# Top-k attention and a low-rank mixer on one core: VectorE and GpSimd put in program order, and some VectorE work moved to GpSimd and ScalarE

## The chip, the cores and the metric

The kernel runs on one core of a Trainium2 chip. A core has TensorE (PE: matmuls, results into PSUM), VectorE (DVE), ScalarE (ACT) and GpSimd (POOL), each with its own instruction queue that is worked off in order, SyncE (SP) which issues most of the DMAs, and SBUF as working memory. Engines wait for one another only through semaphores. The metric is device microseconds of one execution.

## The reference

Eight batches, eight heads, a sequence of 576, a head dimension of 64, all in float32:

```
scores = scale * q @ k^T                       # 576 x 576 per head
kth    = the 32nd largest score of each row
attn   = softmax over the scores >= kth, 0 elsewhere
x      = attn @ v, heads side by side          # (8, 576, 512)
h      = x^T @ U @ V                           # mixes along the sequence, rank 32
u      = x + h^T
out    = u + relu(u @ w_ch1) @ w_ch2           # 512 -> 2048 -> 512
```

U, V, w_ch1 and w_ch2 arrive as float64 and are rounded to float32 in the kernel, by integer operations on their two words.

## The kernel before

The work goes by *pairs* of heads (32 of them, four to a batch) and by *steps*: a pair has five steps, four with 128 rows of queries of both heads (two chunks of 128 x 576 scores) and a fifth with the last 64 rows of both (one chunk). Step n is `divmod(n, 5)`; there are 160.

A step passes these functions. `scores` (from L261 on) computes the scores into PSUM, and ACT copies them to SBUF as `Ssb`. `front` (from L297 on) finds the 32nd largest on VectorE in four rounds: a MAX8 gives the next eight maxima, a MATCH_REPLACE8 strikes them out (L315, L327, L331). The softmax mask of the first chunk is VectorE's (L335), that of the second POOL's (L333, L334), each beside an exponential on ACT (L295; for the second chunk after its mask). `turns` transposes the weights on TensorE (L363, L368), ACT copies them out of PSUM as `PT`. `values` multiplies with v (L383 to L396). When a pair is done, `mixed` transposes its result, scales it by 1/sum into `x` (VectorE, L419, straight out of PSUM), and computes u (pT, Tb, up). When a batch's four pairs are done, `mlp` is appended to the `fillers`: 256 accumulating matmuls, two instructions each in the trace (L467, L486), relu on ACT, and for each of eight tiles the sum `oT` (VectorE, L499, out of PSUM) that `turned_back` transposes, copies to `ob` and stores.

One PSUM pool of two buffers (`ps_t`, tag `tp`) serves all transposes, `O`, `pT` and `up`; another of two serves the MLP.

The order of the work: the main loop runs over the steps and calls these generators in turn. `fill` does a share of MLP matmuls between the pieces of a step, eight times a step; a step of one chunk counts 0.65. The MLP of a batch thus runs beside the attention of the next batch; in the first 21 steps (`n <= ALONE`) there is none to do, and behind the last attention step one batch's MLP is left. `next_params(1)` moves the rounding of weights on by a slab of 128 x 512: it joins the slab before (L160 and L168 on VectorE, L172 on POOL), prepares the one that has arrived (L152, L154 on ACT, L153 on POOL) and loads the next into one of three `raw` buffers. It is called once a step up to step 20 and twice a step after that; there are 36 slabs.

TensorE's and ACT's queues are in the order in which the program calls them:

```python
    ctx.enter_context(tc.manual_schedule(engines={PE, ACT}))
```

The order on VectorE and POOL is that of a scheduler, which takes operations when it thinks them ready, the ones under `high_priority` first; `last_mask` pins a slab's join behind a step's L335 and the next step's first maximum behind the join's first operation.

## Time and profile before

| | |
|---|---|
| runs | 1918.98 us median of 3 (1918.07 to 1920.71) |
| the profiled execution | 1917.73 us, of which the span from first to last instruction is 1915.9 |
| busy of the span | TensorE 1772.1 us, VectorE 1654.0, ACT 953.4, POOL 571.8 |
| granted TensorE clock | 0.958 of full speed, mean |
| the chain that ended last | TensorE 63%, VectorE 26%, ACT 4%, POOL 3% |

The profile is of one execution. "Busy" is time in which an engine had an instruction; the granted clock is that of TensorE, as a share of 2.4 GHz (0.5 is the lower level, 1.2 GHz). A wait is put down to the instruction that ended it. The chain follows the work back from the last instruction, at each point to what released it or to the instruction before it on its engine. Busy shares over the whole span mix stretches with different limits, so the rows further down go by stretch. Line numbers are those of the kernel before.

### The profile page before, as it was taken

The page shows a single profiled execution, that of the slowest core. Times are in us where ns is not written, and L with a number is a line of the kernel's source. Part 1 is how long each engine was busy: PE and PEld are TensorE (multiplying, and loading weights), DVE is VectorE, ACT ScalarE, POOL GpSimd, SP SyncE. Part 2 cuts the span into 40 slices and gives each one's busy share as a digit, 9 for nine tenths or more (in the row PEclk, how much of TensorE's full clock was granted, in tenths as well). Part 3 has the DMA queues.
Part 4 walks back from the last instruction along what each step waited for, and adds up shares of the span by engine and source line. Part 5 has one row for each costly group of instructions (what it writes and reads, how often), then busy time and mean ns, then how long its engine had stood idle before and what let it go on. Part 6 is the DMA issues. An engine that isn't in the chain of part 4 may idle for free.

```text
span 1915.9 us, 29112 instructions
## 1 busy us (share of the span) xinstructions
PE 1772.1 (92%) x10528; PEld 1335.0 (70%) x10528; DVE 1654.0 (86%) x3433; ACT 953.4 (50%) x2345; POOL 571.8 (30%) x346
## 2 busy tenths in 40 slices
PE   5666688999899999999999999999999999999999
PEld 3444465687667877778677877778677877778777
DVE  7999998999999989999899999999899998997000
ACT  4555555554554545555555546555555545554111
POOL 3545556422332222222232222222232222232000
PEclk7767698999999999999999999999999999999999
DMA  2222222201001010100001010101001010000000
GB/s 72 72 60 59 68 74 79 58 17 28 23 20 30 24 30 15 27 18 23 25 20 30 23 31 15 27 15 26 25 20 31 22 31 15 15 8 7 6 14 11
DMA packets 127296, 58.21 MB, mean 30 GB/s; under 512 B 89905, under 2 KB 124977, under 8 KB 127153
## 3 DMA queue, kind: packets, MB, share of 16 engines
q1 hardware_dynamic: 125952, 56.06, 11.0%
q8 instruction: 83, 1.36, 0.3%
q14 instruction: 61, 0.49, 0.1%
q10 hardware_dynamic: 1200, 0.30, 0.1%
HBM read 46.89 MB, written 9.44 MB: 29 GB/s over the span
## 4 chain that ended last, share of the span: by engine, by line
PE 63%; DVE 26%; ACT 4%; issue 3%; POOL 3%; DMA 1%; DVEq 0%; SPq 0%; POOLq 0%; ACTq 0%
PE mm L467 21%; PE mm L486 18%; DVE rr L327 11%; DVE m L331 10%; PE sc L270 6%; PE O L396 5%; PE tp L363 4%; DVE first L315 2%; DVE E L335 2%; PE O L383 1%; PE up L442 1%; ACT E L295 1%; POOL E L333 1%; PE O L393 1%; PE tp L251 1%
## 5 line engine op out<-in xcount | busy, mean ns | idle before, releaser
L331 DVE MAX8 m<-rr 128x8 f32<-128x576 f32 x864 | 614.9, 747 | 4.0
L333 POOL TENSOR_SCALAR E<-Ssb,m 128x576 f32<-128x576 f32 x128 | 285.6, 2231 | 1089.2 <-DVE m L331 546.3
L467 PE MATMUL mm<-uT,w 128*128 128x256 f32 (+1 forms) x2048 | 559.7, 411 | 2.7 <-ACT hT L479 2.7
L486 PE MATMUL mm<-hT,w 128*128 128x256 f32 (+1 forms) x2048 | 560.4, 411 | 0.0
L467 PEld LDWEIGHTS mm<-uT,w 128*128 128x128 f32 x2048 | 364.0, 191 | 110.2 <-issue 30.5
L486 PEld LDWEIGHTS mm<-hT,w 128*128 128x128 f32 x2048 | 364.2, 191 | 100.2 <-issue 22.9
L327 DVE MATCH_REPLACE8 rr<-m,rr 128x576 f32<-128x576 f32 x576 | 427.8, 743 | 0.0
L315 DVE MAX8 first<-Ssb 128x8 f32<-128x576 f32 x288 | 215.6, 752 | 58.6 <-ACT Ssb L290 58.5
L364 ACT COPY PT<-tp 128x512 f32<-128x512 f32 x288 | 168.5, 585 | 187.1 <-PE tp L363 185.2
L363 PE MATMUL tp<-ident,E 128*128 128x128 f32 x1152 | 185.4, 286 | 81.3 <-ACT E L295 54.3
L363 PEld LDWEIGHTS tp<-ident,E 128*128 128x128 f32 x1152 | 144.7, 146 | 145.5 <-ACT E L295 69.1
L295 ACT ACTIVATE E<-Ssb,nmax 128x576 f32<-128x576 f32 x288 | 223.3, 776 | 11.2 <-POOL Ssb L334 5.9
L270 PE MATMUL sc<-qkT 64*128 64x288 f32 (+1 forms) x1280 | 213.9, 457 | 0.4 <-ACT qkT L252 0.4
L327 DVE MATCH_REPLACE8 rr<-first,Ssb 128x576 f32<-128x576 f32 x288 | 212.3, 742 | 0.0
L334 POOL TENSOR_TENSOR Ssb<-Ssb,E 128x576 f32<-128x576 f32 x128 | 188.0, 1469 | 10.6
L405 ACT COPY XT<-O 128x128 f32<-128x128 f32 x128 | 34.2, 267 | 248.9 <-PE O L396 248.9
L479 ACT ACTIVATE hT<-mm 128x320 f32<-128x320 f32 (+1 forms) x256 | 104.3, 408 | 106.7 <-PE mm L467 105.2
L499 DVE TENSOR_TENSOR oT<-uT,mm 128x320 f32<-128x320 f32 (+1 forms) x64 | 28.4, 444 | 146.4 <-PE mm L486 146.4
L396 PE MATMUL O<-PT,va 128*64 128x128 f32 x2048 | 154.2, 298 | 0.0
L270 PEld LDWEIGHTS sc<-qkT 64*128 64x128 f32 (+1 forms) x1280 | 111.2, 189 | 53.9 <-issue 27.3
L335 DVE SCALAR_TENSOR_TENSOR E<-Ssb,m,E 128x576 f32<-128x576 f32 x160 | 130.5, 815 | 18.5 <-ACT E L295 9.9
L396 PEld LDWEIGHTS O<-PT,va 128*64 128x64 f32 x2048 | 120.7, 147 | 17.1 <-issue 3.6
(68 smaller groups left out, 1378.1 us busy)
## 6 DMA issues: line engine op xcount, KB each, us to landing
raw<-in_moe_w_ch_dram SPq DMA_DIRECT2D x32, 512.0 KB, 3.8
ld_q<-in_q_dram SPq DMA_DIRECT2D x64, 128.0 KB, 2.8
va<-in_v_dram SPq DMA_DIRECT2D x64, 128.0 KB, 2.4
out_dram<-ob SPq DMA_DIRECT2D x64, 128.0 KB, 1.9
ld_k<-in_k_dram SPq DMA_DIRECT2D x62, 128.0 KB, 2.8
ld_ends<-in_q_dram SPq DMA_DIRECT2D x32, 32.0 KB, 2.2
vd<-in_v_dram SPq DMA_DIRECT2D x64, 16.0 KB, 2.0
vt<-in_v_dram SPq DMA_DIRECT2D x32, 32.0 KB, 2.3
```

Source lines behind the costliest of these rows:

```text
L270: nc.tensor.matmul(sc[slice(0, n) if t < NT else half(h), h, 0:HALF], lhsT=qkT[half(h), 0, cols(t)], rhs=qkT[half(h), 1, i * HALF : (i + 1 ...
L295: nc.scalar.activation(E, chunk, AF.Exp, bias=nmax, scale=SCALE, accum_out=total)
L315: ins = nc.vector.max(ms[c], curs[c])
L327: nc.vector.match_replace(nxt, ms[c], curs[c], NEG)
L331: nc.vector.max(ms[c], curs[c])
L333: nc.gpsimd.tensor_scalar(Es[1], chunks[1], ms[1][:, 7:8], NEG, ALU.is_lt, ALU.mult)
L334: nc.gpsimd.tensor_tensor(chunks[1], chunks[1], Es[1], ALU.add)
L335: ins = nc.vector.scalar_tensor_tensor(out=Es[0], in0=chunks[0], scalar=ms[0][:, 7:8], in1=Es[0], op0=ALU.is_ge, op1=ALU.mult, accum_out=s ...
L363: nc.tensor.transpose(tp[:, j, :], E2[:, a : a + P], ident)
L396: nc.tensor.matmul(O[half(h)], lhsT=va[:, h, j, :], rhs=PT[:, NT * h + j], start=False, stop=(j == NT - 1),)
L467: nc.tensor.matmul(ph[:, 0:w], lhsT=w1[:, cc, f * P : (f + 1) * P], rhs=uT[:, cc, lo:hi], start=(cc == 0), stop=(cc == NC - 1),)
L486: nc.tensor.matmul(po[:, 0:w], lhsT=w2[:, f, c * P : (c + 1) * P], rhs=hTs[f][:, 0:w], start=(f == 0), stop=(f == NF - 1),)
```

## The change

VectorE and POOL are now also in program order; the scheduler places nothing. A step's rounds are given out in pieces: `front` yields after each round, and the main loop calls the pieces at set places, with `fill`, `next_params` and the transposes between them. Up to step 20, a step's transposes and its product with v come one step later than before.

Three pieces of work move. The scaling of `x` is now a copy out of PSUM on ACT and a product on POOL. The sum `oT` is a copy on ACT and a sum on POOL, but for the last batch, which stays on VectorE; its turned-back transposes come after ten matmuls of the next tile (before: four) or behind the fourth hidden tile (before: the second). The join of a slab has one VectorE operation, a shift; the second, which put sign and exponent in, becomes a Sign activation on ACT and an integer sum on POOL. At the start, the second halves of q and k are loaded on ACT's queue (before: all of k), and two of the first copies are VectorE's.

```diff
@@ -65,6 +65,7 @@
     PE, ACT = mybir.EngineType.PE, mybir.EngineType.Activation
+    DVE, POOL = mybir.EngineType.DVE, mybir.EngineType.Pool
     const = ctx.enter_context(tc.tile_pool(name="const", bufs=1))
@@ -74,7 +75,7 @@
     ps_m = ctx.enter_context(tc.tile_pool(name="ps_m", bufs=2, space=bass.MemoryType.PSUM))
-    ctx.enter_context(tc.manual_schedule(engines={PE, ACT}))
+    ctx.enter_context(tc.manual_schedule(engines={PE, ACT, DVE, POOL}))
     PARTS = ((0, 1, NT), (2, 3))
@@ -151,23 +156,17 @@
         nc.gpsimd.tensor_scalar(bits.bitcast(F32), bits.bitcast(F32), TINY, None, ALU.max)
-        nc.scalar.activation(low, low8, AF.Identity, bias=half_bit[0:n], scale=1.0 / 32)
+        nc.scalar.activation(low, low8, AF.Identity, bias=step[0:n], scale=(1 + 2.0**-10) / 32)
+        nc.scalar.activation(hi.bitcast(F32), hi.bitcast(F32), AF.Sign, bias=nudge[0:n])
         return hi, bits, low
     def f64_join(hi, bits, low, outs):
-        ins = nc.vector.tensor_scalar(
-            bits, bits, 3, 0x3FFFFFFF, ALU.logical_shift_left, ALU.bitwise_and
-        )
-        if last_mask:
-            tc.add_manual_dep(ins.ins, last_mask[-1], mybir.DependencyInfo(
-                mybir.DependencyClass.NoSync, mybir.DependencyReason.DATA
-            ), reason="order")
-        nc.vector.scalar_tensor_tensor(
-            out=bits, in0=hi, scalar=0xC0000000, in1=bits, op0=ALU.bitwise_and, op1=ALU.bitwise_or
-        )
+        nc.vector.tensor_single_scalar(bits, bits, 3, ALU.logical_shift_left)
+        nc.gpsimd.tensor_tensor(bits, bits, hi, ALU.add)
         for dst, form in outs:
@@ -220,14 +219,14 @@
         for name, src in (("q", q), ("k", k)):
-            queue = nc.scalar if g == 0 and name == "k" else nc.sync
             t = loads.tile([P, NT, 2, D], F32, tag=f"ld_{name}", name=f"ld_{name}")
             for i in range(2):
+                queue = nc.scalar if g == 0 and i else nc.sync
                 queue.dma_start(
...
                 )
-            queue.dma_start(
+            nc.sync.dma_start(
                 ends[half(len(tiles))], src[b, h0 : h0 + 2, MAIN:S, :].rearrange("h p d -> p h d")
@@ -249,7 +248,8 @@
                 nc.tensor.transpose(tp[:, c, :], t[:, c].rearrange("p h d -> p (h d)"), ident)
-            nc.scalar.copy(qkT[:, i, 0:MAIN], tp.rearrange("p t n -> p (t n)"))
+            copy = nc.vector.tensor_copy if g == 0 and i else nc.scalar.copy
+            copy(qkT[:, i, 0:MAIN], tp.rearrange("p t n -> p (t n)"))
             yield
@@ -285,7 +285,8 @@
         last = S2[:, MAIN : MAIN + 2 * TAIL].rearrange("p (h n) -> p h n", h=2)
-        nc.scalar.copy(main[:, :, 0:HALF], scs[0][:, :, 0:HALF])
+        copy = nc.vector.tensor_copy if g + t == 0 else nc.scalar.copy
+        copy(main[:, :, 0:HALF], scs[0][:, :, 0:HALF])
         nc.scalar.copy(main[:, :, HALF:MAIN], scs[1][:, :, 0 : MAIN - HALF])
@@ -312,16 +313,12 @@
             ms[c] = first[:, c]
-            ins = nc.vector.max(ms[c], curs[c])
-            if last_mask:
-                tc.add_manual_dep(ins.ins, last_mask.pop(), mybir.DependencyInfo(
-                    mybir.DependencyClass.NoSync, mybir.DependencyReason.DATA
-                ), reason="order")
+            nc.vector.max(ms[c], curs[c])
         yield
-        nc.scalar.mul(nmax[:, 0:n], first[:, 0:n, 0], -SCALE)
-        weigh(chunks[0], Es[0], nmax[:, 0:1])
         for i in range(1, TOPK // 8):
+            if i == 1:
+                nc.scalar.mul(nmax[:, 0:n], first[:, 0:n, 0], -SCALE)
+                weigh(chunks[0], Es[0], nmax[:, 0:1])
             for c in order:
@@ -329,10 +326,11 @@
                 nc.vector.max(ms[c], curs[c])
+            yield
         if n == 2:
...
             nc.gpsimd.tensor_tensor(chunks[1], chunks[1], Es[1], ALU.add)
-        ins = nc.vector.scalar_tensor_tensor(
+        nc.vector.scalar_tensor_tensor(
             out=Es[0],
@@ -341,7 +339,6 @@
         )
-        last_mask.append(ins.ins.name)
         if t == NT:
@@ -376,9 +373,8 @@
             den, x = dens[g], xs[g % 2]
-            with tc.high_priority():
-                nc.vector.tensor_scalar_add(den, den, 1e-9)
-                nc.vector.reciprocal(den, den)
+            nc.vector.tensor_scalar_add(den, den, 1e-9)
+            nc.vector.reciprocal(den, den)
             for j in range(NT + 1):
@@ -415,13 +411,11 @@
             nc.tensor.transpose(tp[:, t, :], XT[:, cols(t)], ident)
-        with tc.high_priority():
-            nc.vector.tensor_tensor(
-                X[:, 0:NT, :].rearrange("p t (h d) -> p t h d", h=2),
-                tp.rearrange("p t (h d) -> p t h d", h=2),
-                den[:, 0 : 2 * NT].rearrange("p (t h) -> p t h ()", h=2).to_broadcast([P, NT, 2, D]),
-                ALU.mult,
-            )
+        X4 = X[:, 0:NT, :].rearrange("p t (h d) -> p t h d", h=2)
+        tp4 = tp.rearrange("p t (h d) -> p t h d", h=2)
+        den4 = den[:, 0 : 2 * NT].rearrange("p (t h) -> p t h ()", h=2).to_broadcast([P, NT, 2, D])
+        nc.scalar.copy(X4, tp4)
+        nc.gpsimd.tensor_tensor(X4, X4, den4, ALU.mult)
         for _ in range(wait):
@@ -477,7 +471,7 @@
                 nc.scalar.activation(hTs[f][:, 0:w], ph[:, 0:w], AF.Relu)
-                if f == 1 and late:
+                if f == 3 and late:
                     late.pop()()
@@ -490,13 +484,16 @@
                     )
-                    if f == 3 and late:
+                    if f == 9 and late:
                         late.pop()()
...
                 oT = mlpp.tile([P, WIDE], F32, tag="oT", name="oT")
-                with tc.high_priority():
+                if b == B - 1:
                     nc.vector.tensor_tensor(oT[:, 0:w], uT[:, c, lo:hi], po[:, 0:w], ALU.add)
+                else:
+                    nc.scalar.copy(oT[:, 0:w], po[:, 0:w])
+                    nc.gpsimd.tensor_tensor(oT[:, 0:w], oT[:, 0:w], uT[:, c, lo:hi], ALU.add)
                 late.append(turned_back(b, chunks, lo, c, oT))
@@ -567,30 +564,42 @@
             next(fronts[n])
+        here, last = fronts.get(n, iter(())), fronts.pop(n - 1, iter(()))
         if n <= ALONE:
+            next(turning, None)
+            next(turning, None)
             scores(*divmod(n + 1, CH))
-            if n:
+            fill()
+            if n >= 2:
+                values(*divmod(n - 2, CH))
+            if n >= 1:
                 turning = turns(*divmod(n - 1, CH))
-            next(turning, None)
-            next(fronts[n])
-            if n:
-                next(fronts.pop(n - 1))
+            if n == ALONE:
+                next(turning)
+                next(turning)
+                next(here)
+                values(*divmod(n - 1, CH))
+                mixing.append(mixed((n - 1) // CH, 0))
+                while mixing:
+                    fill()
+            else:
+                next(here)
             next_params(1)
+            if n and n < ALONE:
+                next(turning)
+            fill()
+            next(last, None)
             next(ready, None)
+            next(here)
             fill()
-            next(turning, None)
+            if n >= 2 and (n - 2) % CH == NT:
+                mixing.append(mixed((n - 2) // CH, 3))
+            next(here)
+            next(here)
             fill()
-            next(turning, None)
-            if n:
-                values(*divmod(n - 1, CH))
-                if (n - 1) % CH == NT:
-                    mixing.append(mixed((n - 1) // CH, 1))
-            while mixing:
-                fill()
-            for _ in range(3):
-                fill()
             continue
+        next_params(1)
         fill()
@@ -602,21 +611,21 @@
             scores(*divmod(n + 1, CH))
-        if n < STEPS:
-            next(fronts[n])
+        next(here, None)
         if n - 2 >= ALONE and (n - 2) % CH == NT:
...
         fill()
+        next(here, None)
+        fill()
         next_params(1)
-        fill()
         if n <= STEPS:
...
         fill()
-        if n <= STEPS:
-            next(fronts.pop(n - 1))
-        fill()
-        next_params(1)
+        next(here, None)
+        next(last, None)
+        next(here, None)
+        fill()
     while mixing or fillers:
```

On VectorE, around the first pair's `x`. Before, step 5 (`first` is a step's first maximum, `m` a later round's, `rr` the scores with maxima struck out):

```order
L160 TENSOR_SCALAR uT<-uT 128x64
L315 MAX first<-Ssb 128x8
L380 TENSOR_SCALAR den<-den 128x9
L168 SCALAR_TENSOR_TENSOR uT<-raw,uT 128x64
L381 RECIPROCAL den<-den 128x9
L327 MATCH_REPLACE rr<-first,Ssb 128x576 x2
L331 MAX m_596<-rr 128x8
L331 MAX m_598<-rr 128x8
L327 MATCH_REPLACE rr<-m_596,rr 128x576
L315 MAX first<-Ssb 128x8
L419 TENSOR_TENSOR x_97<-tp,den 128x512
L327 MATCH_REPLACE rr<-m_598,rr 128x576
```

With the change, from the end of step 5 into step 6:

```order
L333 SCALAR_TENSOR_TENSOR E,den<-Ssb,m_630,E 128x576
L316 MAX first<-Ssb 128x8 x2
L376 TENSOR_SCALAR den<-den 128x9
L377 RECIPROCAL den<-den 128x9
L324 MATCH_REPLACE rr<-first,Ssb 128x576 x2
L328 MAX m_669<-rr 128x8
L328 MAX m_671<-rr 128x8
L168 TENSOR_SCALAR w_107<-w_107 128x512
L324 MATCH_REPLACE rr<-m_669,rr 128x576
L324 MATCH_REPLACE rr<-m_671,rr 128x576
L328 MAX m_701<-rr 128x8
L328 MAX m_703<-rr 128x8
```

The second operation of the join and `x` are gone from VectorE; the shift stands between the rounds, and the two first maxima stand together.

On POOL, where two slabs are rounded in a step, from the mask of step 22 (L333 before, L331 with the change) to that of step 23. Before:

```order
L333 TENSOR_SCALAR E<-Ssb,m_2151 128x576
L153 TENSOR_SCALAR w_108<-w_108 128x4x128
L334 TENSOR_TENSOR Ssb<-Ssb,E 128x576
L172 TENSOR_TENSOR w_108<-w_108,raw 128x4x128 x2
L153 TENSOR_SCALAR w_108<-w_108 128x4x128 x2
L333 TENSOR_SCALAR E<-Ssb,m_2264 128x576
L334 TENSOR_TENSOR Ssb<-Ssb,E 128x576
```

With the change:

```order
L331 TENSOR_SCALAR E<-Ssb,m_2213 128x576
L332 TENSOR_TENSOR Ssb<-Ssb,E 128x576
L169 TENSOR_TENSOR w_108<-w_108,raw 128x4x128
L171 TENSOR_TENSOR w_108<-w_108,raw 128x4x128
L158 TENSOR_SCALAR w_108<-w_108 128x4x128
L169 TENSOR_TENSOR w_108<-w_108,raw 128x4x128
L171 TENSOR_TENSOR w_108<-w_108,raw 128x4x128
L158 TENSOR_SCALAR w_108<-w_108 128x4x128
L331 TENSOR_SCALAR E<-Ssb,m_2326 128x576
L332 TENSOR_TENSOR Ssb<-Ssb,E 128x576
```

A slab has three POOL operations in place of two (L158 was L153, L171 was L172, L169 is new), and the two slabs of a step stand apart in their own order.

On TensorE, the turned-back transposes of one tile in the second batch (`mm` are the MLP's sums, `sc` scores). Before:

```order
L486 MATMUL mm<-hT,w_108 128x320 x2
L393 MATMUL O<-PT,vd_92 128x128
L396 MATMUL O<-PT,va_89 64x128 x8
L270 MATMUL sc<-qkT 128x288 x4
L486 MATMUL mm<-hT,w_108 128x320 x2
L511 MATMUL tp<-ident,oT 128x128 x2
L511 MATMUL tp<-ident,oT 64x128
L363 MATMUL tp<-ident,E 128x128 x4
L486 MATMUL mm<-hT,w_108 128x320 x4
```

With the change:

```order
L480 MATMUL mm<-hT,w_108 128x320 x2
L389 MATMUL O<-PT,vd_92 128x128
L392 MATMUL O<-PT,va_89 64x128 x8
L270 MATMUL sc<-qkT 128x288 x4
L480 MATMUL mm<-hT,w_108 128x320 x2
L360 MATMUL tp<-ident,E 128x128 x4
L480 MATMUL mm<-hT,w_108 128x320 x4
L360 MATMUL tp<-ident,E 128x128 x4
L480 MATMUL mm<-hT,w_108 128x320
L365 MATMUL tp<-ident,E 128x128
L480 MATMUL mm<-hT,w_108 128x320
L508 MATMUL tp<-ident,oT 128x128 x2
L508 MATMUL tp<-ident,oT 64x128
```

The transposes of `oT` stand behind ten matmuls of the next tile in place of four; the matmuls themselves and the attention's places among them are the same.

## Rows read from the trace of the kernel before

**Rows 1.** Stretches: length, busy PE, PEld, DVE, ACT, POOL (x instructions), clock, DMA, GB/s.
```profile
0.00:247.00 247.00, 154.93 (x810) 103.62 (x811) 222.71 (x472) 126.75 (x293) 118.14 (x90) 0.70 0.24 66
247.00:360.00 113.00, 96.11 (x508) 66.17 (x508) 103.00 (x205) 64.80 (x147) 72.06 (x45) 0.94 0.29 82
360.00:475.00 115.00, 112.23 (x724) 89.44 (x724) 110.95 (x227) 60.28 (x151) 33.91 (x20) 1.00 0.09 23
475.00:564.00 89.00, 81.72 (x516) 59.02 (x515) 87.50 (x186) 48.71 (x121) 25.36 (x14) 1.00 0.09 23
564.00:781.00 217.00, 212.10 (x1316) 161.45 (x1315) 204.59 (x427) 113.59 (x284) 57.96 (x32) 1.00 0.09 23
781.00:997.00 216.00, 212.34 (x1319) 161.75 (x1317) 202.31 (x421) 113.98 (x285) 57.92 (x32) 1.00 0.09 24
1645.00:1786.00 141.00, 139.79 (x867) 110.09 (x867) 112.65 (x234) 66.85 (x171) 32.61 (x18) 1.00 0.03 8
1786.00:1916.00 130.00, 125.91 (x530) 98.36 (x528) 3.63 (x8) 16.72 (x44) 0.00 (x0) 1.00 0.04 11
```

**Rows 2.** VectorE's waits until 247 us: us in total, times, longest.
```profile
DVE first L315 <- ACT Ssb L290: 10.9, 1, 10.9
DVE x L419 <- PE tp L417: 9.1, 4, 2.8
```

**Rows 3.** The chain, 70 to 93 us: start, us, what.
```profile
70.74 0.69 DVE x L419
...
78.33 0.59 DVE w L168
```

**Rows 4.** The chain, 223 to 250 us.
```profile
223.93 2.30 POOL E L333
...
247.15 2.96 PE mm L467 x11
```

**Rows 5.** Waits from 247 to 360 us.
```profile
POOL w L153 <- ACT w L152: 36.0, 13, 6.0
ACT w L152 <- DMA raw<-in_moe_w_ch_dram: 15.3, 6, 5.3
...
PE tp L363 <- ACT E L295: 11.8, 5, 6.3
```

**Rows 6.** TensorE in a regular batch: start, us, instructions [idle before <-releaser].
```profile
920.45 0.66 PE L363 MATMUL tp<-ident,E 128*128 128x128 f32 x4 [1.58 <-DVE x L419]
...
930.12 0.41 PE L511 MATMUL tp<-ident,oT 128*128 128x128 f32 x2 [1.76 <-DVE oT L499]
```

**Rows 7.** VectorE until 224 us, line 168: busy us, mean ns | idle before.
```profile
L168 DVE SCALAR_TENSOR_TENSOR w<-raw,w 128x512 uint32<-128x512 uint32 x13 | 8.7, 666 | 0.0
```

**Rows 8.** Groups of instructions: two ACT copies out of PSUM.
```profile
L364 ACT COPY PT<-tp 128x512 f32<-128x512 f32 x288 | 168.5, 585 | 187.1 <-PE tp L363 185.2
...
L452 ACT COPY uT<-up 128x320 f32<-128x320 f32 x64 | 25.6, 399 | 35.7 <-PE up L444 35.7
```

**Rows 9.** POOL in a regular batch.
```profile
911.19 1.41 POOL L334 TENSOR_TENSOR Ssb<-Ssb,E 128x576 f32<-128x576 f32 x1
```

**Rows 10.** POOL from 247 to 360 us, by line.
```profile
L153 POOL TENSOR_SCALAR w<-w 128x512 f32<-128x512 f32 x15 | 23.4, 1557 | 36.0 <-ACT w L152 36.0
L172 POOL TENSOR_TENSOR w<-w,raw 128x512 uint32<-128x512 uint32 x15 | 19.8, 1340 | 1.9 <-DVE w L168 1.9
L333 POOL TENSOR_SCALAR E<-Ssb,m 128x576 f32<-128x576 f32 x8 | 19.3, 2410 | 8.9 <-DVE m L331 8.9
L334 POOL TENSOR_TENSOR Ssb<-Ssb,E 128x576 f32<-128x576 f32 x7 | 10.6, 1511 | 0.5
```

**Rows 11.** ACT in a regular batch.
```profile
921.62 0.78 ACT L295 ACTIVATE E<-Ssb,nmax 128x576 f32<-128x576 f32 x1
```

**Rows 12.** POOL where slabs are joined.
```profile
226.32 1.92 POOL L334 TENSOR_TENSOR Ssb<-Ssb,E 128x576 f32<-128x576 f32 x1
...
259.74 2.94 POOL L333 TENSOR_SCALAR E<-Ssb,m 128x576 f32<-128x576 f32 x1
```

More of the change, by code (lines that the diff above doesn't have):

```diff
@@ L104 @@
     V = const.tile([NT * R, S], F32, name="V")
-    half_bit = const.tile([P, 1], F32, name="half_bit")
-    nc.vector.memset(half_bit, 1.0 / 64)
+    step = const.tile([P, 1], F32, name="step")
+    nc.vector.memset(step, 2.0**23)
+    nudge = const.tile([P, 1], F32, name="nudge")
+    nc.vector.memset(nudge, 0.4 * TINY)
     def rows(t):
@@ L120 @@
     SLAB = 512
-    spare, last_mask = [], []
+    spare = []
     def f64_raw(srcs):
```

## The prediction

> **What bounds the kernel now.** I read the stretches first [rows 1]. They split the run in three. Until 247 us TensorE runs at a granted clock of 0.70 (a mean of time at 1.2 and at 2.4 GHz), is busy for 155 us of 247, and VectorE is busy for 223: this is batch 0's attention, with no MLP to fill TensorE. From 247 us on there is MLP work, and TensorE is busy nearly all the time: the idle time left is 16.9 us to 360, 2.8 to 475, 7.3 to 564, 4.9 to 781, then 3.7 in each of four stretches of 216 us (one stands in the rows, the three behind it read alike), 1.2 to 1786 and 4.1 in the tail, where VectorE has nothing left to do. That is 52 us of idle in 1669; the other 1617 are matmuls that the change neither adds to nor takes from. So the time is (when the MLP starts) + 1617 + (TensorE's idle time after that), less what a faster clock gives back, and I ask of each edit which of the three it moves.
>
> Next, what delays the MLP start. VectorE's waits until 247 us are two that matter: 10.9 us for the first scores, and four waits of together 9.1 us in front of x, line 419 [rows 2]. Beyond these it is saturated, so up to the last steps of batch 0 what VectorE does in its queue is the path; the chain shows the pieces, 0.69 us for x and 0.59 us for line 168 of one slab [rows 3]. Then the chain leaves VectorE at 223.93, with the mask of step 18, and reaches the first MLP matmul at 247.15: 23.2 us over POOL, ACT and TensorE [rows 4].
>
> Last, who makes TensorE idle later. From 247 to 360, while two slabs of weights are rounded in each step, ACT waits 15.3 us for the raw slab's DMA, and TensorE 11.8 us for ACT's exponentials behind that [rows 5]; ACT evicts everything TensorE makes, so what holds its queue holds TensorE. In the regular batches the 3.7 us are two stalls: 1.58 us of a transpose that needs the PSUM buffer which x reads, and 1.76 us of the turned-back transposes that wait for oT [rows 6]. In both the operation was ready and stood in VectorE's queue behind a round.
>
> **Part by part.** The sum is made against the profiled execution, 1917.73 us with a span of 1915.9; the median of the runs, 1918.98, is 1.25 above it.
>
> *A, until the MLP starts.* Line 168 goes to POOL. By 224 us 13 full slabs have passed it, 8.7 us busy [rows 7]; in the chain one costs 0.59 us, so 13 make 7.7, and the four small slabs about 1: 8.7 us. x goes to ACT and POOL: three of its four stand before 224 us, so 3/4 of 9.1 us of waiting and 3 x 0.69 of work, 8.9 us. VectorE no longer steps aside for TensorE there; the two small operations on den stay. The rounds themselves are the same instructions; in program order a step's first maximum no longer slips between the rounds of the step before, which costs nothing on a saturated engine. The start of the kernel (loads on two queues, two copies on VectorE in place of ACT) I take as 0, between -1 and +1: a copy of this size on ACT is 0.59 us [rows 8], and k's first half now queues behind q's on SP. On the 23.2 us behind the last mask: x costs a copy of about 0.6 and a POOL product of about 1.4 [rows 8, 9] in place of 0.69, +1.3; against that the slab's ACT operations now stand in front of the exponential that waits for the mask, not behind it. I take 0, between -2 and +3. What hides the rest is slack: POOL's step in batch 0 is now mask, product and three slab operations, 2.4 + 1.5 + 1.6 + 1.3 + 1.3 = 8.1 us by the dearer rows [rows 10], under VectorE's step of 11 (223 us for some 20 steps); if POOL were over it, the surplus would come 18 times. Sum: -17.6; the MLP starts at about 229.6.
>
> *B, 247 to 360.* Here each step has two joins. Before, both stand together behind a step's last VectorE operation, the raw buffers come free in one bunch, and the next two loads land late; that is the wait of 15.3 us. Now one join stands behind the first maximum and one behind the second round, half a step apart, and the load that follows is issued half a step earlier than its ACT operation needs it. Against it POOL has 2 x 1.34 us more in each step: 2 x (1.56 + 1.34) + 2.41 + 1.51 = 9.7 becomes 12.4 [rows 10], 8.5 in a step of one chunk; eight steps are 7 x 12.4 + 8.5, and 1.4 for x, 97 us. TensorE's pace, 216 us for 20 steps in which a one-chunk step counts 0.65, is 11.6 and 7.5 us, 89 us for the eight. So POOL falls back by up to 8 us. It has about that much in hand: in a regular step the mask is done at 912.60 and its exponential runs at 921.62, 9.0 us later [rows 9, 11]. Of the 16.9 us of idle I keep 6, between 0 and 25. The clock there is 0.94 over 96 us busy, 5.8 us lost; with fewer stalls I take half back, 3 us. Sum: -13.9.
>
> *C, 360 to 564.* 10.1 us of idle. Between the MLP of batch 0 and that of batch 1 there are two steps without MLP work in both orders, and TensorE then waits for VectorE. VectorE is now less loaded, but TensorE arrives there less delayed. I keep 8: -2, between -8 and +3.
>
> *D, 564 to 1645, five batches with 4.9 + 4 x 3.7 = 19.7 us of idle.* For x TensorE now needs only ACT's copy, 0.59 us in a queue that is half idle; the product on POOL is due four pieces of filling later. For oT the way is a copy of about 0.4 [rows 8] and a POOL sum of about 0.8 (1.41 x 320/576 columns [rows 9], less for 256), against a wait that is now 1.76. I expect 0.3 + 0.7 to stay per batch, 6 in five: -13.7, between -19.7 and +10. The other turned-back tiles are due after ten matmuls instead of four, so the longer way is covered by five more microseconds of matmuls; if POOL were still in a mask, 2.4 + 1.5 = 3.9 us [rows 10], they could be late. VectorE's own savings here (x 0.69 four times, oT eight times in a batch) are off the path.
>
> *E, behind 1645.* 5.3 us of idle, the last batch's oT stays on VectorE: 0.
>
> Sum: -17.6 - 13.9 - 2 - 13.7 = -47; 1917.7 - 47 = 1870.5, so 1871 us.
>
> **A rule against it.** The sum operation on POOL beside VectorE takes 1.92 us at 226 us, where a slab is being joined, and 1.41 at 911, where none is [rows 9, 12]; the maxima beside either have the same length. The Trainium skill, "Perfetto Trace Analysis", Optimizing Scalar/DVE Operations, says that GpSimd and VectorE share an SBUF read port, "so offloading operations between those two might not help". The two lengths agree with a shared port; by the rule the moved work comes back as longer POOL operations, and that is the second rival. The trace speaks for less than that, since line 168 itself, with two inputs, is what goes.
>
> **Rivals.**
> 1. *Only the start gains.* The two-hop hand-overs (ACT, then POOL) keep TensorE waiting as long as x and oT did, and the idle of B is that of the clock and of step lengths: B, C and D are 0, 1917.7 - 17.6 = 1900. For it: every hop passes two in-order queues. Against it: both queues are idle half the time there.
> 2. *POOL is the bound in the eight steps.* With the longer lengths of the two mask operations, 2.9 and 1.9 [rows 12], and 2 x 4.2 for the slabs, 13.2 us a step, 7 x 13.2 + 8.5 + 1.4 = 102 against 89: 13 us, of which the slack no longer covers much, since ACT's exponential blocks all evictions behind it. B turns from -14 to +6 or so: 1890.
> 3. *Slower.* In the regular batches POOL's queue is in program order: an oT sum or an x product that stands behind a mask waits for VectorE's last round, then 3.9 us for the mask, with TensorE at the turned-back transposes waiting for it. There are 12 such hand-overs in a batch, 84 in seven. Against a gain of 47 us it decides from 0.56 us on the mean of them. With three full masks in a batch it is 7 x 3 x 3.9 = 82 us: 1953. Against it: VectorE leads in the regular steps, the mask is over 9 us before it is wanted.
> 4. *No change*: the MLP start hangs on loads and ACT rather than on VectorE, and the rest cancels: 1918. Hardly, as the first 224 us of the chain are VectorE's.
>
> **Chances.** Forecast 0.60, in its own range 1856 to 1885; rival 1 0.16, rival 2 0.13, rival 3 0.07, rival 4 0.04. The range for 8 in 10 is 1850 to 1900: its low end is all idle of B and D gone and the clock back (17.6 + 16.9 + 5.8 + 19.7 = 60, and some of C), its high end is rival 1. A measurement here can tell 0.2%, 3.8 us, from no change: faster 0.90, the same 0.03, slower 0.07.
>
> **What would show it.** Right: the first MLP matmul at 227 to 233 us; no VectorE wait for TensorE in batch 0 beside the first; ACT's wait for raw slabs under 5 us; granted clock from there to 340 us above 0.95; TensorE busy over 214 of 216 us in the regular batches, with waits on POOL under 1 us. Wrong: a VectorE wait for POOL in the slab's shift (then POOL is the bound in A or B); "PE waited for POOL" at the turned-back transposes or in front of pT, several in each batch; or POOL's products near 2 us all through.

## The result and the profile after

| | before | after |
|---|---|---|
| runs, median | 1918.53 us (1917.87 to 1920.71, 4 runs) | 1876.95 us (1876.64 to 1877.13, 4 runs) |
| span of the profiled execution | 1915.9 | 1875.0 |
| start of the first MLP matmul | 246.94 | 233.11 |
| from there to the end | 1669.0 | 1641.9 |
| the chain that ended last | TensorE 63%, VectorE 26% | TensorE 80%, VectorE 1%, followed back to 280 us only |

The ratio is 0.978, with a 95% interval of 0.976 to 0.980: 42 us faster. The forecast was 1871, with a range of 1850 to 1900. 13.8 us came before the MLP start (17.6 forecast) and 27.1 behind it (29.6 forecast). (The 247.15 of [rows 4] is where the chain enters that matmul; its row begins at 246.94, and all starts here are those of the rows.) The two chains can't be compared: the one after breaks off at a DMA at 280 us, so it says nothing of the first 233 us, in which VectorE is still busy for 218. Of all runs below, one of the kernel with x back was in a slower state of the chip (1925.67 us at a granted clock of 0.918); it and its trace are left out.

The stretches of the kernel after, cut at the same points of the work as [rows 1] (columns as there; line numbers here and below are those of the kernel that a row is from):

```profile
0.00:233.00 233.00, 137.97 (x808) 92.54 (x809) 218.09 (x455) 136.02 (x313) 137.43 (x114) 0.75 0.26 70
233.00:340.00 107.00, 96.30 (x534) 66.19 (x532) 93.97 (x191) 76.90 (x169) 95.79 (x66) 0.97 0.28 85
340.00:455.00 115.00, 115.00 (x744) 92.64 (x744) 108.91 (x223) 64.90 (x164) 37.00 (x25) 1.00 0.09 25
455.00:530.00 75.00, 68.12 (x417) 48.68 (x414) 73.31 (x150) 43.28 (x106) 23.80 (x14) 0.95 0.11 26
530.00:740.00 210.00, 208.96 (x1293) 159.29 (x1292) 199.28 (x407) 117.38 (x293) 68.44 (x44) 1.00 0.09 23
740.00:953.00 213.00, 211.96 (x1319) 161.47 (x1320) 199.62 (x409) 119.09 (x297) 68.93 (x44) 1.00 0.09 24
1745.00:1875.00 130.00, 125.96 (x530) 98.36 (x528) 3.64 (x8) 16.73 (x44) 0.00 (x0) 1.00 0.04 11
```

Read the second column against the first: TensorE's idle time is 10.7 us in the first 107 us of MLP work, 0 in the next 115, 6.9 around the change from batch 0's MLP to batch 1's, and 1.04 in each regular batch, which now takes 213 us instead of 216. POOL, 95.8 us busy of 107 in the second line, is the fullest engine beside TensorE there.

VectorE's waits until 247 us (us in total, times, longest):

```profile
DVE qkT L252 <- PE tp L250: 6.0, 1, 6.0
DVE w L168 <- POOL w L158: 4.1, 2, 2.2
DVE Ssb L289 <- PE sc L270: 1.8, 1, 1.8
DVE first L316 <- ACT Ssb L291: 0.9, 1, 0.9
```

The 10.9 us for the first scores are three waits of 8.7 in all, and the four waits in front of x [rows 2] are gone. A new one has come, the shift of a slab waiting for POOL; both times it is behind the MLP start.

TensorE's waits from 225 us to the end:

```profile
PE pT L424 <- POOL x L418: 8.1, 3, 3.2
PE tp L508 <- POOL oT L496: 5.5, 6, 1.3
PE tp L360 <- ACT E L296: 5.3, 10, 1.5
```

The exponentials' 11.8 us of [rows 5] have shrunk to 5.3 over the whole rest, 4.0 of it until 340 us; the two ways over POOL have come in.

POOL from 233 to 340 us, by line (busy, mean ns | idle before, and what ended it), against [rows 10]:

```profile
L158 POOL TENSOR_SCALAR w<-w 128x512 f32<-128x512 f32 x16 | 24.4, 1523 | 2.9 <-ACT w L157 2.9
L171 POOL TENSOR_TENSOR w<-w,raw 128x512 uint32<-128x512 uint32 x16 | 21.1, 1319 | 1.3
L331 POOL TENSOR_SCALAR E<-Ssb,m 128x576 f32<-128x576 f32 x8 | 18.0, 2255 | 0.0
L332 POOL TENSOR_TENSOR Ssb<-Ssb,E 128x576 f32<-128x576 f32 x7 | 9.9, 1412 | 0.6
```

None is longer than before; the mask's sum is 1.41 us here as in a regular batch.

Last, VectorE and POOL around den in step 6 (start, us, instructions):

```profile
72.94 1.42 DVE L316 MAX8 first<-Ssb 128x8 f32<-128x576 f32 x2
...
73.88 1.40 POOL L332 TENSOR_TENSOR Ssb<-Ssb,E 128x576 f32<-128x576 f32 x1
74.28 1.03 DVE L376 TENSOR_SCALAR den<-den 128x9 f32<-128x9 f32 x1
75.34 0.21 DVE L377 RECIPROCAL den<-den 128x9 f32<-128x9 f32 x1
```

The addition to den, 128 x 9 numbers, takes 1.03 us. In the kernel before each of the 32 took 0.15 to 0.17, with POOL idle beside them. It ends 0.03 us after POOL's sum (75.31 and 75.28). So do the 24 of the 32 that begin while POOL is in that sum, L332: they last 1.02 to 1.11 us and end within 0.06 us of it. Six stand beside POOL's L331, a TENSOR_SCALAR, and two beside an idle POOL; these take 0.15 to 0.17.

### The profile page after: what moved, and what is told of

The parts are those of the page before. It is cut to its first block, busy times and chain, and to the rows that moved or that the text cites. A ratio compares the mean times of both kernels' runs of the same rounds, so it can differ in the third digit from the quotient of the medians.

```text
span 1875.0 us, 29258 instructions
## 1 busy us (share of the span) xinstructions
PE 1751.8 (93%) x10528; PEld 1321.8 (70%) x10528; DVE 1617.5 (86%) x3312; ACT 1009.0 (54%) x2467; POOL 684.9 (37%) x470
## 4 chain that ended last, share of the span: by engine, by line
PE 80%; ACT 3%; POOL 1%; DVE 1%; issue 1%; DMA 0%; POOLq 0%; ACTq 0%; DVEq 0%
PE mm L480 26%; PE mm L461 25%; PE sc L270 8%; PE O L392 6%; PE tp L360 6%; PE O L379 2%; PE up L436 2%; PE O L389 1%; PE tp L250 1%; PE tp L508 1%; PE up L438 1%; PE pT L424 1%; PE tp L365 1%; PE tp L413 1%; ACT E L296 1%
## 5 line engine op out<-in xcount | busy, mean ns | idle before, releaser
L331 POOL TENSOR_SCALAR E<-Ssb,m 128x576 f32<-128x576 f32 x128 | 286.6, 2239 | 594.1 <-DVE m L328 482.2
L316 DVE MAX8 first<-Ssb 128x8 f32<-128x576 f32 x288 | 205.3, 750 | 0.9 <-ACT Ssb L291 0.9
L333 DVE SCALAR_TENSOR_TENSOR E<-Ssb,m,E 128x576 f32<-128x576 f32 x160 | 134.8, 843 | 68.2 <-ACT E L296 51.7
L332 POOL TENSOR_TENSOR Ssb<-Ssb,E 128x576 f32<-128x576 f32 x128 | 180.5, 1410 | 10.7
L392 PE MATMUL O<-PT,va 128*64 128x128 f32 x2048 | 142.5, 282 | 0.0
L496 POOL TENSOR_TENSOR oT<-oT,uT 128x320 f32<-128x320 f32 (+1 forms) x56 | 45.0, 803 | 236.9 <-ACT oT L495 235.2
L493 DVE TENSOR_TENSOR oT<-uT,mm 128x320 f32<-128x320 f32 (+1 forms) x8 | 3.6, 455 | 146.2 <-PE mm L480 146.2
```

Source lines behind the costliest of these rows:

```text
L316: nc.vector.max(ms[c], curs[c])
L331: nc.gpsimd.tensor_scalar(Es[1], chunks[1], ms[1][:, 7:8], NEG, ALU.is_lt, ALU.mult)
L332: nc.gpsimd.tensor_tensor(chunks[1], chunks[1], Es[1], ALU.add)
L392: nc.tensor.matmul(O[half(h)], lhsT=va[:, h, j, :], rhs=PT[:, NT * h + j], start=False, stop=(j == NT - 1),)
```

## The experiments

Twelve kernels ran, each timed against the kernel before on its chip. From their traces, the start of the first MLP matmul and what the span leaves behind it:

| kernel | median us | ratio to before, 95% | MLP start | from there on |
|---|---|---|---|---|
| before | 1918 | | 246.9 | 1669.0 |
| order alone | 1896.3 | 0.987 to 0.990 | 243.4 | 1650.7 |
| join back | 1892.0 | 0.985 to 0.988 | 243.9 | 1646.4 |
| x back | 1876.7 | 0.977 to 0.980 | | |
| oT back | 1874.2 | 0.976 to 0.978 | 233.4 | 1640.3 |
| after | 1876.95 | 0.976 to 0.980 | 233.1 | 1641.9 |
| scheduled | 1987.2 | 1.034 to 1.037 | 237.0 | 1748.5 |
| turns early | 1881.4 | 0.979 to 0.982 | 234.0 | 1645.6 |
| without 1e-9 | 1871.7 | 0.974 to 0.977 | 230.2 | 1640.7 |
| den earlier | 1869.4 | 0.973 to 0.976 | 231.1 | 1637.7 |
| in place | 1871.0 | 0.974 to 0.976 | 229.7 | 1639.3 |
| spread | 1874.3 | 0.976 to 0.978 | 233.9 | 1638.7 |
| four edits | 1859.7 | 0.967 to 0.970 | 227.9 | 1631.4 |
| five edits | 1862.2 | 0.969 to 0.972 | 229.1 | 1631.5 |

### Undoing one part: x, oT, the join, the order

**x back on VectorE.**

```diff
-        nc.scalar.copy(X4, tp4)
-        nc.gpsimd.tensor_tensor(X4, X4, den4, ALU.mult)
+        nc.vector.tensor_tensor(X4, tp4, den4, ALU.mult)
```

> The changed kernel with x back on VectorE, straight out of PSUM, at the same place of the program. Theory (x counts twice): in batch 0 VectorE steps aside for TensorE's transposes again, 1.5 to 2.8 us and 0.7 of work at three of the four pairs before the last mask, so that mask comes 8 us later and the MLP starts at about 241 instead of 233; in the regular batches TensorE's transposes wait for a PSUM buffer that x still has to read, 1.2 us in each of six batches, 7 more: 1892 us, between 1886 and 1896. Rival (the order did it, x alone is worth nothing): in program order x stands at a place where its transposes are done, under 3 us in all: 1877 to 1880.

Measured 1876.7 us, 0.2 below the changed kernel: beside the rest of the change the move of x is worth nothing. The rival holds.

**oT back on VectorE** in all batches.

```diff
-                if b == B - 1:
                     nc.vector.tensor_tensor(oT[:, 0:w], uT[:, c, lo:hi], po[:, 0:w], ALU.add)
-                else:
-                    nc.scalar.copy(oT[:, 0:w], po[:, 0:w])
-                    nc.gpsimd.tensor_tensor(oT[:, 0:w], oT[:, 0:w], uT[:, c, lo:hi], ALU.add)
```

> The changed kernel with the sum oT on VectorE in all batches, straight out of PSUM; the turned-back transposes stay behind ten matmuls. Theory (the later place covers it): a sum is at most one round (2.9 us) late and the ten matmuls are longer, so TensorE's stalls stay away; VectorE has 14 us in a batch of 213 to spare and needs 8 x 0.45 us and eight waits for TensorE: 1879 us, between 1876 and 1884. Rival 1 (moving oT was what took the stall away): TensorE waits 1.5 us for oT in each of six batches again, 1887. Rival 2: in its order VectorE waits some 2 us at each of the eight and becomes the bound of the batch: 6 x 5 us or more, over 1900.

1874.2 us, 2.7 below the changed kernel and at the low end of the theory. A regular batch has 0.4 us of TensorE idle instead of 1.04. Moving oT was a small loss.

**The join back**: both operations on VectorE, no Sign, no POOL sum for them.

```diff
...
-        nc.scalar.activation(low, low8, AF.Identity, bias=step[0:n], scale=(1 + 2.0**-10) / 32)
-        nc.scalar.activation(hi.bitcast(F32), hi.bitcast(F32), AF.Sign, bias=nudge[0:n])
+        nc.scalar.activation(low, low8, AF.Identity, bias=half_bit[0:n], scale=1.0 / 32)
...
-        nc.vector.tensor_single_scalar(bits, bits, 3, ALU.logical_shift_left)
-        nc.gpsimd.tensor_tensor(bits, bits, hi, ALU.add)
+        nc.vector.tensor_scalar(
+            bits, bits, 3, 0x3FFFFFFF, ALU.logical_shift_left, ALU.bitwise_and
+        )
+        nc.vector.scalar_tensor_tensor(
+            out=bits, in0=hi, scalar=0xC0000000, in1=bits, op0=ALU.bitwise_and, op1=ALU.bitwise_or
+        )
```

> The changed kernel with the old join: two operations on VectorE (shift with mask, then sign and exponent put in), no Sign on ACT and no sum on POOL for them. Theory (the second operation is the term A says it is): 0.65 us more on VectorE for each of 13 slabs before the last mask, 8.5 us, and POOL's masks take 1.9 us beside it again; the MLP starts at 241 to 243, and from 233 to 340 the idle time of TensorE is the same 11 us or a few less, since POOL has 2.7 us less in a step: 1884 us, between 1880 and 1888. Rival (POOL's extra sum costs as much as it saves): the MLP start and the stretch behind it cancel, within 3 us of 1877.

1892.0 us, 15.0 more than the changed kernel, above the theory's range: right in kind, too small in size. The mask of step 18 on POOL, where before's chain leaves VectorE [rows 4], in this kernel and then in the changed one:

```profile
223.65 2.22 POOL L332 TENSOR_SCALAR E<-Ssb,m 128x576 f32<-128x576 f32 x1 [2.44 <-DVE m L329]
```

```profile
212.30 2.22 POOL L331 TENSOR_SCALAR E<-Ssb,m 128x576 f32<-128x576 f32 x1 [1.08 <-DVE m L328]
```

With the join back the mask stands where it stood before, at 223.9. A normal step of VectorE (one with two chunks and no den), from mask to mask, takes 11.93 us here, 11.20 in the changed kernel: 0.73 a slab, more than line 168's 0.59 in the old chain. The rows of one join show where the 0.14 lie, in the kernel before and then here:

```profile
88.89 0.42 DVE L160 TENSOR_SCALAR w<-w 128x512 uint32<-128x512 uint32 x1
89.22 0.75 DVE L315 MAX8 first<-Ssb 128x8 f32<-128x576 f32 x1
89.89 0.67 DVE L168 SCALAR_TENSOR_TENSOR w<-raw,w 128x512 uint32<-128x512 uint32 x1
90.48 0.09 DVE L327 MATCH_VALUE_LOAD rr<-first,Ssb 128x8 f32 x1
```

```profile
205.26 0.41 DVE L165 TENSOR_SCALAR w<-w 128x512 uint32<-128x512 uint32 x1
205.70 0.69 DVE L168 SCALAR_TENSOR_TENSOR w<-raw,w 128x512 uint32<-128x512 uint32 x1
206.31 0.08 DVE L325 MATCH_VALUE_LOAD rr<-m,rr 128x8 f32 x1
```

Behind a shift the maximum starts after 0.33 us, line 168, which reads what the shift writes, after 0.44; and from line 168 to the next start it is 0.61 for 0.59: together 0.13.

**The order alone**: the three edits above together. What is left of the change is not the queues' order only: the loads and copies at the start and the later places of the turned-back transposes stay too.

> The order alone: the changed kernel's order on all four engines, with x, oT and both operations of the join back on VectorE. Theory (the order takes TensorE's stalls away, the join's move is the only move that pays): the single undoings add up, 1892 with the join back and -3 with oT back, so 1889 us, between 1885 and 1894, with the MLP starting at 244 and one us or less of idle time in a regular batch of 213. Rival (each move is only worth nothing because the others leave VectorE the room): with all of it back VectorE is behind in the regular batches and x and oT make TensorE wait again, 3 us a batch: 1900 to 1910.

1896.3 us, between theory and rival. Its stretches behind the MLP start and in a regular batch, and two of VectorE's waits from 740 to 1592 us, four batches:

```profile
243.00:350.00 107.00, 92.69 (x508) 63.42 (x507) 104.95 (x197) 65.61 (x148) 67.48 (x46) 0.98 0.29 85
...
750.00:963.00 213.00, 212.07 (x1320) 161.90 (x1319) 205.68 (x421) 114.45 (x286) 57.88 (x32) 1.00 0.10 25
```

```profile
DVE oT L492 <- PE mm L480: 8.3, 8, 1.1
...
DVE x L418 <- PE tp L414: 2.0, 4, 0.5
```

The second line is the finding: 0.93 us of TensorE idle in a batch of 213, with x and oT straight from PSUM on VectorE as before. TensorE's two waits for VectorE of [rows 6] are gone, and the roles have changed: VectorE waits for TensorE there, 0.5 to 1.1 us at a time, no longer TensorE for VectorE. (0.72 of the 0.93 stand at the same turned-back transposes, put down to an ACT copy, that of qkT.) From 243 to 350 the order takes no idle time away: VectorE is busy 105 of 107 us, and TensorE is idle for 14.3 us, as it was in the same 107 us before (14.2). There the moved work pays. With x and oT gone from VectorE and the join still on it, 9.3 us of idle are left (the kernel with the join back, 244 to 351 us), 5 less, and the two kernels differ by 4.3 us. So x and oT are worth 4.3 us as long as VectorE has the join; once it is rid of it, each alone is worth nothing or less (0.2 and 2.7 us faster with it back; both back beside the new join did not run).

Taken one after the other, order, then x and oT, then the join: 22.1 + 4.3 + 15.0 = 41.4 of the 41.6 us. Of the 13.8 us before the MLP start the order has 3.6, the join 10.8, and x and oT cost 0.6.

**The moved work in the scheduler's order.**

```diff
-    ctx.enter_context(tc.manual_schedule(engines={PE, ACT, DVE, POOL}))
+    ctx.enter_context(tc.manual_schedule(engines={PE, ACT}))
```

> The changed kernel with VectorE and POOL in the scheduler's order again; all work stays where the change put it. Theory (the moved work carries the gain, the order little): what used to stand behind a round on VectorE is no longer on VectorE, so the order costs 3 us, between -3 and +8: 1880. Rival (the order carries half or more of it): VectorE's first maxima and POOL's slab operations slip in front of what the step needs, MLP start 240 or later and idle time of 20 us or more from there to 340: 1895 to 1915.

1987.2 us: slower than before by 3.6%, and both expectations far off. TensorE's longest wait from 740 to 1592 us, and one batch:

```profile
PE pT L424 <- POOL x L418: 38.2, 15, 3.0
```

```profile
744.00:957.00 213.00, 201.85 (x1233) 154.11 (x1232) 181.22 (x378) 108.94 (x272) 65.46 (x42) 0.98 0.09 24
```

POOL around one of these products, whose copy on ACT was done at 826.91:

```profile
826.57 2.21 POOL L331 TENSOR_SCALAR E<-Ssb,m 128x576 f32<-128x576 f32 x1 [6.01 <-DVE m L328]
828.86 1.49 POOL L332 TENSOR_TENSOR Ssb<-Ssb,E 128x576 f32<-128x576 f32 x1
830.31 1.04 POOL L418 TENSOR_TENSOR x<-x,den 128x512 f32<-128x512 f32 x1
```

This is the prediction's rival 3, in another kernel: x's product stands in POOL's queue behind a mask that waited for VectorE's last round, TensorE stands at pT, 11 of these 213 us are idle, and a batch takes 228 us instead of 213. The change also takes away the priority that x and oT had; whether the scheduler would have put the products earlier with it was not tried. In this order the kernel is 69 us slower than before, in the program's 42 faster.

### Where the turned-back transposes stand

```diff
-                if f == 3 and late:
+                if f == 1 and late:
...
-                    if f == 9 and late:
+                    if f == 3 and late:
```

> The changed kernel with the turned-back transposes at their old places, after four matmuls of the next tile or the second hidden tile, while oT keeps its way over ACT and POOL. Theory (the later place covers the longer way): four matmuls, some 2.2 us, don't cover ACT's copy, POOL's sum and a mask of 3.6 us that may stand in front of it; 48 tiles, a third of them late by 1 to 2 us: 1895 us, between 1885 and 1915, and TensorE's waits for POOL's oT over 15 us. Rival (POOL is idle two thirds of the time there and in time after four as well): 1877 to 1880.

1881.4 us, +4.4, the rival nearly. In a regular batch TensorE loses 1.15 us instead of 1.04; 3.0 us come from 234 to 456 us, 1.7 of them up to 341, while slabs still pass POOL. In the regular batches four matmuls cover the way over ACT and POOL as well as ten. They could not gain much there: these places had no wait before either. The 1.76 us of [rows 6] stand at the last tile of a batch, once in each, and its transposes come when the tile is done, which no kernel here changes. The same place in the changed kernel:

```profile
898.37 0.44 PE L508 MATMUL tp<-ident,oT 128*128 128x128 f32 x2 [0.83 <-POOL oT L496]
```

### den and POOL's sum

**den one step earlier**, where POOL has no mask to work off.

```diff
-            nc.vector.tensor_scalar_add(den, den, 1e-9)
-            nc.vector.reciprocal(den, den)
...
+        if t == 0 and 0 < n <= STEPS:
+            den = dens[g - 1]
+            nc.vector.tensor_scalar_add(den, den, 1e-9)
+            nc.vector.reciprocal(den, den)
```

> The changed kernel with den's addition and reciprocal one step earlier on VectorE, behind the two first maxima of the next pair's first step, where the step before had one chunk and POOL has no mask to work off. Theory (in the changed kernel den's addition waits until POOL's sum of the mask, its TENSOR_TENSOR, has ended): the addition takes 0.15 us instead of 1.03, three pairs before the mask of step 18, so that mask and the MLP start come 2.7 us earlier, at 230.4: 1874.3 us, between 1873 and 1876. Rival (a small operation behind the first maxima costs 1 us wherever it stands): the addition stays at 1.03 and the time at 1877.

1869.4 us, 7.6 less. The addition takes 0.15 us and the steps with den 11.48 instead of 12.36; the mask of step 18 comes 2.7 us earlier, the MLP start 2.0. Of the 6.2 us between the two spans the other 4.2 lie behind the MLP start and were not foreseen: the hole where the MLP changes batches shrinks by 1.6 us and TensorE keeps its clock in it (1.00 for 0.95); the rest is spread over small differences.

**Without den's addition** (the 1e-9 is left out).

```diff
-            nc.vector.tensor_scalar_add(den, den, 1e-9)
```

> The changed kernel without den's addition (the 1e-9 is left out); the reciprocal stands where both stood. Theory (the wait is that of the addition's form, TENSOR_SCALAR, against POOL's TENSOR_TENSOR): the reciprocal takes 0.2 us although POOL is in its sum at the same moment; steps 6, 11 and 16 take 11.4 instead of 12.4 us, the MLP starts 3 us earlier: 1874 us. Rival 1 (whatever reads den first there waits, for den's last piece or behind the maxima): the reciprocal takes 1.0 us, 1876 to 1877. Rival 2 (POOL's sum holds up every VectorE operation but the maxima): the same 1.0 us.

1871.7 us, and step 6 again:

```profile
73.72 1.40 POOL L332 TENSOR_TENSOR Ssb<-Ssb,E 128x576 f32<-128x576 f32 x1
74.11 0.20 DVE L376 RECIPROCAL den<-den 128x9 f32<-128x9 f32 x1
```

The reciprocal stands in the middle of POOL's sum, reads the same den, and takes 0.20 us; so it does in all 23 places of this run where it begins in that sum (0.19 to 0.20). So neither the place nor the data makes the addition wait: its form against POOL's sum does. Both rivals fall.

### Towards a faster kernel

**Strike-outs in place**, so that the later rounds need no third `rr` buffer.

```diff
-                nxt = attn.tile([P, S], F32, tag="rr", name="rr", bufs=3)
+                nxt = curs[c]
+                if i == 1:
+                    nxt = attn.tile([P, S], F32, tag="rr", name="rr", bufs=3)
```

> The changed kernel with the strike-outs of the later rounds written over their own input, so that a step needs two rr buffers and never waits for a third. Theory (in the second and third round the second MATCH_VALUE_LOAD starts 0.12 us late because its output buffer is the one that the strike-out in front of it has just read): 0.24 us less in each full step, 16 of them before the mask of step 18, so the MLP starts 3.8 us earlier and a normal step takes 10.96 instead of 11.20 us: 1873 us, between 1872 and 1875. Rival (the 0.12 us is the wait for the maximum itself): steps of 11.20 and 1877.

1871.0 us, 6.0 less, with normal steps of 10.95 us and the MLP start 3.4 us earlier: the theory, with 2 us more behind the MLP start, which it did not have. One round in the changed kernel and in this one:

```profile
90.08 0.74 DVE L324 MATCH_REPLACE8 rr<-m,rr 128x576 f32<-128x576 f32 x1
90.85 0.09 DVE L324 MATCH_VALUE_LOAD rr<-m,rr 128x8 f32 x1
```

```profile
88.38 0.73 DVE L326 MATCH_REPLACE8 rr<-m,rr 128x576 f32<-128x576 f32 x1
89.04 0.07 DVE L326 MATCH_VALUE_LOAD rr<-m,rr 128x8 f32 x1
```

From the start of a strike-out to that of the next load it was 0.77 us and is 0.66. No wait view lists the 0.11 us; in the rows it shows only as this difference.

**The MLP of batch 0 spread** over the steps there are for it.

```diff
-    def fill(n=1):
+    def fill(k=1):
...
-        for _ in range(n):
+        slow = 0.93 if n < 2 * ALONE + 2 else 1
+        for _ in range(k):
...
-            due += share * (SHORT if t == NT else 1)
+            due += slow * share * (SHORT if t == NT else 1)
```

> The changed kernel with batch 0's share of the MLP spread over the 21.5 steps that there are for it (0.93 of the share up to step 41) in place of 20. Theory (the hole at 455 to 530, 6.9 us of idle and a clock of 0.95, is two steps without MLP work): the hole goes, idle there 1 us, clock 1.0: 1868 us, between 1866 and 1872. Rival (a slower pace of TensorE only hands the bound to VectorE and ACT): the idle time moves into 233 to 455, 1875 to 1879.

1874.3 us, 2.7 less. The same three stretches as in the changed kernel, from its MLP start:

```profile
234.00:341.00 107.00, 94.55 (x531) 64.55 (x531) 92.19 (x189) 79.82 (x174) 97.29 (x67) 0.98 0.28 84
341.00:456.00 115.00, 112.80 (x728) 89.31 (x727) 112.20 (x230) 64.16 (x162) 35.21 (x24) 1.00 0.09 24
456.00:531.00 75.00, 73.01 (x446) 53.24 (x445) 73.31 (x150) 44.27 (x108) 24.51 (x15) 1.00 0.12 28
```

The hole is 2.0 us instead of 6.9 and the clock 1.00, but 1.8 and 2.2 us of idle came back in the two stretches before: theory and rival both hold, half and half. Behind the MLP start TensorE's idle time falls by 0.9 us in all (28.1 to 27.2) and its busy time by 2.4 (1613.8 to 1611.4), so most of the gain is in shorter matmuls, with the clock at 1.00 for 0.95 in the hole.

**Four of them together**: den earlier, in place, spread, oT back.

> Four of the single edits together: den one step earlier, strike-outs in place, batch 0's MLP spread over 21.5 steps, oT on VectorE in all batches. Theory (each has its own place: VectorE before the MLP start, the hole at 455 to 530, the regular batches): the single gains add up, 7.6 + 6.0 + 2.7 + 2.8 = 19: 1858 us, between 1855 and 1864; MLP start at 227 to 228, under 1 us of idle time in a regular batch. Rival (several of the single gains were the same hole and the same clock in it): 1865 to 1869.

1859.7 us, 17 less than the changed kernel and 3.1% (2.97 to 3.26) below the one before: the single gains add up but for 2 us. It beats both kernels.

**A fifth**: up to step 16 the last round's maxima in the other order.

```diff
-            for c in order:
+            for c in order if i < 3 or g * CH + t > 16 else order[::-1]:
                 ms[c] = small.tile([P, 8], F32, tag="m8", name="m8", bufs=8)
```

> The same four edits, and up to step 16 the last round's two maxima in the other order, that of VectorE's own mask first. Theory (VectorE's mask, a SCALAR_TENSOR_TENSOR, stands 0.13 us waiting for the maximum just in front of it): 13 full steps are 0.13 us shorter, 1.7 us in all, MLP start at 226: 1856 us, between 1853 and 1862. Rival (POOL gets its mask 0.7 us later in every step, and the slab's sums behind it): the same as the kernel beside it or up to 3 us more.

1862.2 us, 2.5 more: the rival, by the same collision as den's. POOL's mask comes later, its sum meets the shift, VectorE's other TENSOR_SCALAR, and holds it until 57.25 (two more shifts, at 107.83 and 159.91, take 1.55 us instead of 0.41 in the same way; the steps they stand in are 1.1 us longer):

```profile
55.84 1.41 POOL L334 TENSOR_TENSOR Ssb<-Ssb,E 128x576 f32<-128x576 f32 x1
```

```profile
55.99 1.32 DVE L168 TENSOR_SCALAR uT<-uT 128x64 uint32<-128x64 uint32 x1
```

## Why the prediction was right, and where not

The time is 6 us above the forecast, inside its own range of 1856 to 1885, and the frame held: MLP start 233.1 + TensorE's busy 1613.9 + its idle time 28 = 1875.

**A, -17.6 forecast, -13.8 measured.** The mask of step 18 came 11.6 us earlier, what follows up to the MLP is 20.8 us instead of 23.0 (0 forecast), and the first maximum begins 0.6 us earlier (11.12 for 11.73; 0 forecast for the start). Of its two terms line 168 was under-sized, 8.7 forecast, 11.35 measured between the kernel with the join back and the changed one. The term of x, 8.9, failed. That VectorE "no longer steps aside for TensorE" is true, but the order did it: in the kernel with the order alone x waits 0.6 us in all before the MLP. And the order took as much again elsewhere: its mask of step 18 stands at 225.79, later than before (223.93). Moving x and oT brings that mask 2.1 us earlier (223.65 with the join back), x's own work, and what follows becomes longer by 2.7 (17.6 to 20.3 us); the prediction had put that second term at 0. The step that failed is "in program order a step's first maximum no longer slips between the rounds of the step before, which costs nothing on a saturated engine". It costs: a normal step with both join operations takes 11.65 us before and 11.93 in program order, because that maximum had stood between the two join operations, and between the strike-outs that share a buffer (by the rows above 0.13 and 0.11 of the 0.28); and den's operations, which "stay", went from 0.16 to 1.03 us at three pairs.

**B, idle 16.9 to 6 forecast, 10.7 measured.** ACT's wait for the raw slabs fell from 15.3 us to 2.8 (under 5 forecast), and the clock rose from 0.94 to 0.97, as taken. POOL's lengths were right: mask and two slabs of L158, L169 (1.30) and L171 are 2.26 + 1.41 + 2 x 4.14 = 11.95 us a step, 12.4 forecast, against TensorE's 11.6. So rival 2 holds in part: the shift waits 11.1 us for POOL in eight places, the mark that was to show POOL as the bound, and TensorE waits 2.8 us for x. Its longer lengths did not come: the mask's sum is 1.41 us on the mean, not 1.9. The rule beside it, in the Trainium skill, "Perfetto Trace Analysis", Optimizing Scalar/DVE Operations, that moving work between the two engines might not help, did not come true for this operation: moving the join's second operation from VectorE to ACT and POOL brought 15 us.

**C, -2 forecast, -3.2 measured.** The spread kernel shows that the hole is the two steps without MLP work.

**D, 19.7 to 6 forecast, 5.2 measured** (1.0 and four times 1.04). The size is right, and so is what the way over ACT and POOL leaves at oT, 0.83 us a batch for 0.7; the reason is not. The prediction put the gain on x and oT leaving VectorE; with both back there the kernel with the order alone leaves 0.93 us a batch. What had been wrong is where they stood in VectorE's queue, behind a round, as the profile said; I took the way out that the diff offered for the one that worked. The five more us of matmuls as cover weren't needed either: in the regular batches of the kernel before none of the tiles they cover waited.

**E, 0 forecast, 0.1 measured**: 5.4 us of idle for 5.3. The rest of the gain is TensorE's busy time behind the MLP start, 1617.2 us before and 1613.9 after, with the better clock of B (3 forecast).

**Rival 3** stayed away by the order that this change brings with it, and came in the kernel without that order: with the same work moved, the place in POOL's queue makes the difference.

## What to carry over

When an operation was ready but stood behind a long one in its queue, try another place in that queue first: here the stall was gone by that. Moving the operation to other engines is a second question, and here only the join's move paid by itself. Undo each part of a change alone and all together: x and oT were worth 4.3 us beside the old join and nothing, each alone, without it. Where two engines work side by side, look at small operations whose length has changed and at what ends with them: moving one addition per pair, 0.9 us too long in 24 of 32, was worth 7.6 in the end. And before reading shares of the chain, see how far back it goes.

## What was not expected of the hardware

A TENSOR_SCALAR of VectorE that begins in POOL's TENSOR_TENSOR ended with it or just behind: 24 of 24 den additions of the changed kernel (1.02 to 1.11 us instead of 0.15), its two shifts that did so (1.26 and 1.08 us instead of 0.41, ending 0.28 behind POOL's operation), and the small shift in the last kernel (1.32 instead of 0.17). The wait lies inside the instruction's own time and no wait view lists it, so semaphores are not all that engines here wait for. A TENSOR_SCALAR of POOL didn't hold up den (six additions at 0.15 to 0.16), and VectorE's RECIPROCAL runs in 0.20 us beside POOL's sum. The slab's shift beside a TENSOR_SCALAR of POOL is not settled: 0.40 to 0.43 us in six of seven meetings of the changed kernel and 0.66 in the seventh, but 0.82 to 0.89 in five of the kernel before, three of which ended 0.28 us behind POOL's operation. The Trainium skill, "SBUF — State Buffer", Who interferes with whom, has VectorE's tensor_scalar among the operations that can take the pair of ports shared with GpSimd, and a GpSimd operation hold that pair for its whole length. The 24 agree with it; the six beside POOL's one-input operation do not.

Nothing here settles why den and the strike-outs in place gain behind the MLP start as well as before it. With den earlier TensorE's idle time there falls by 2.8 us and its busy time by 1.4; with the strike-outs in place the idle time stays (28.3 us for 28.1) and the busy time falls by 2.8, at a granted clock of 1.00 for 0.97 in the first 107 us.
